# Decode attention with a gated MLP: all heads' scores of a batch in two PSUM banks, one softmax per batch

## The chip, the cores and the metric

One core of a Trainium2 chip runs the whole kernel. The metric is the device time of one execution in microseconds (us). The engines are PE (matmul and transpose), DVE, ACT, POOL and SP, which here only issues the loads.

## What is computed

Four sequences (B) with one token each, width 576 (D). 32 query heads share 16 key/value heads (KVH) of size 128, two query heads to one. Attention looks at the last 4096 positions (WIN) of a cache of 16384. All inputs are bf16.

```python
h  = x + softmax(q @ k.T * DH**-0.5) @ v @ wo        # q = layernorm(x) @ wq, per batch and head
g  = layernorm(h) @ W_gate                           # 576 x 4608
h2 = h + (relu(g) * (layernorm(h) @ W_up)) @ W_down  # 4608 x 576
```

K and V of the window are 64 pairs (batch, kv head) of 1 MB each; with the weights (wq, wo, gate, up, down, 4.5 to 5.3 MB each) the core reads 159.58 MB.

## The kernel before

The loop runs over the 64 pairs. For a pair `i`, K arrives as 128 partitions of 32 rows of 128 values. `do_tr` (line 582) transposes its 32 blocks on PE into four PSUM banks of 8 blocks each; `evac` (line 332) copies each bank to `kT_pool`, three on DVE (line 342) and the fourth on ACT (line 344). `do_qk` (line 601) has the blocks of kT as stationary operand and two columns of q as moving one: 32 matmuls of 2 columns, so the scores lie with positions on partitions, 128 x 64 in a bank. `dve_rmax` (line 469) reduces them to 128 x 2, POOL makes the maximum over partitions with `partition_all_reduce` (line 427) and scales it (line 429), `act_exp` (line 384) makes the exponentials of each of the two heads with that bias. `do_pv` (line 622) has the blocks of V as stationary operand and two columns of probabilities as moving one: 32 matmuls at line 633.

PE's order for step `i` is: transposes of pair i, QK of pair i-1, PV of pair i-3. The transposes into a bank wait for that bank's copy of the pair before; ACT's queue holds the copy of pair i and then the exponentials of pair i-1. POOL's two instructions per pair stand in order on its queue.

All loads go through SP's queue in one order: x, wq in five chunks of 128 (the last of 64) input rows, then K(m) and V(m-3) alternating, the four parts of wo among them, then gate and up by chunks of input rows, then down in five parts. K, wq, gate and up share a ring of 7 slots, V and down another of 7; a load waits for the instruction that reads the slot's last content (`add_transfer`, line 237). A wait at the head of SP's queue holds all later loads.

After the loop come `wo` (160 matmuls with 4 columns, line 661), the second layernorm, gate and up (360, line 682), the product, down (180, line 699), a transpose back and one output DMA (line 353).

Of the kernel before, what the change touches and what calls it, by code (L numbers as in the profile page):

```python
# [7 lines left out]
ALU = mybir.AluOpType  # L8
# [4 lines left out]
B = 4  # L13
# [6 lines left out]
T = WIN // 128  # L20
F = 4608
FC = F // 128
# [5 lines left out]
NSTREAM = 14  # L28
NWO = 4
SLOT = 4608  # L30
NKT = 3
NSB = 2
LAGQ = 1
LAGP = 2
NP = 4
NM = 4
NRA = 7
VLEAD = 3
WO_AFTER = 4
KT_BANK0 = 4  # L40
EVAC_ENG = ("vector", "vector", "vector", "scalar")

# [7 lines left out]
class Ev:  # L50
    __slots__ = ("key", "val")

    def __init__(self, key, val):
        self.key = key
        self.val = val


class Sched:
    def __init__(self):
        self.emit = False  # L60
        self.sem_keys = []
        self._keyset = set()
        self.sems = {}
        self.engines = {}
        self.named = {}
        self.rec_hist = {}
        self.begin_pass(False)
        for e in ENGS:
            self._key("cnt_" + e)

    def _key(self, key):
        if key not in self._keyset:
            assert not self.emit, ("semaphore key discovered in emit pass", key)
            self._keyset.add(key)
            self.sem_keys.append(key)

    def begin_pass(self, emit, nc=None, es=None):
        self.emit = emit
        self.counters = {e: 0 for e in ENGS}
        self.dma_counts = {}  # L80
        self.waited = {}
        self.rec_idx = {}
        if not emit:
            self.rec_hist = {}
            self.named = {}
        else:
            for key in self.sem_keys:
                self.sems[key] = es.enter_context(nc.semaphore("s_" + key))
            self.engines = {
                "sync": nc.sync,  # L90
                "scalar": nc.scalar,
                "vector": nc.vector,
                "gpsimd": nc.gpsimd,
                "tensor": nc.tensor,
            }

    def record(self, name, ev):
        if self.emit:
            idx = self.rec_idx.get(name, 0)
            self.rec_idx[name] = idx + 1  # L100
            hist = self.rec_hist.get(name)
            assert hist is not None and idx < len(hist), ("event not seen in pass 1", name)
            old = hist[idx]
            assert old.key == ev.key and old.val == ev.val, ("event mismatch", name)
        else:
            self.rec_hist.setdefault(name, []).append(ev)
        self.named[name] = ev
        return ev

    def get(self, name):  # L110
        ev = self.named.get(name)
        if ev is None:
            if self.emit:
                raise KeyError(name)
            return None
        return ev

    def wait(self, eng, ev):
        if ev is None:
            return  # L120
        k = (eng, ev.key)
        if self.waited.get(k, -1) >= ev.val:
            return
        self.waited[k] = ev.val
        if self.emit:
            self.engines[eng].wait_ge(self.sems[ev.key], ev.val)

    def op(self, eng, thunk, deps=()):
        for d in deps:
            self.wait(eng, d)  # L130
        key = "cnt_" + eng
        self._key(key)
        self.counters[eng] += 1
        val = self.counters[eng]
        if self.emit:
            ins = thunk(self.engines[eng])
            ins.then_inc(self.sems[key], 1)
        return Ev(key, val)

    def dma(self, eng, thunk, sem_key, deps=(), val=None):  # L140
        for d in deps:
            self.wait(eng, d)
        self._key(sem_key)
        self.dma_counts[sem_key] = self.dma_counts.get(sem_key, 0) + 16
        if val is None:
            val = self.dma_counts[sem_key]
        if self.emit:
            ins = thunk(self.engines[eng])
            ins.then_inc(self.sems[sem_key], 16)
        return Ev(sem_key, val)  # L150


def bass_sequential_preLN__sliding_block_cached__glu_gated_reglu__decode_kernel(
# [12 lines left out]
    with ExitStack() as es:  # L166
        cnt = [0]

        def sb(shape, dt):
            cnt[0] += 1  # L170
            return es.enter_context(nc.sbuf_tensor(f"sbt{cnt[0]}", shape, dt))

        def ps(shape, dt):
            cnt[0] += 1
            return es.enter_context(nc.psum_tensor(f"pst{cnt[0]}", shape, dt))

        pool = sb([128, NSTREAM + NWO, SLOT], BF16)
        kT_pool = sb([128, NKT, WIN], BF16)
        ident_b = sb([128, 128], BF16)
        ident_f = sb([128, 128], FP32)  # L180
        ones_f = sb([128, 128], FP32)
        eps_c = sb([128, 1], FP32)
        x_bf = sb([B, D], BF16)
        x_f = sb([B, D], FP32)
        junk_f = sb([B, D], FP32)
        xn_bf = sb([B, D], BF16)
        st1 = sb([B, 16], FP32)
        xnT = sb([128, DC, B], BF16)
        xT = sb([128, DC, B], FP32)
        qT_sb = sb([128, B, H], BF16)  # L190
        pmax = sb([128, NM, 2], FP32)
        bcm = sb([128, NM, 2], FP32)
        nb = sb([128, NM, 2], FP32)
        probT = sb([128, NP, T, 2], BF16)
        rowsum = sb([128, B, H], FP32)
        rs_sb = sb([128, H], FP32)
        oT_all = sb([128, H, B], BF16)
        R_sb = sb([128, 2, DC, B], FP32)
        st2 = sb([128, 40], FP32)
        tmp5 = sb([128, DC, B], FP32)  # L200
        hnT = sb([128, DC, B], BF16)
        acc = sb([128, 2, FC, B], FP32)
        hhT = sb([128, FC, B], BF16)
        h2T = sb([128, DC, B], FP32)
        out_sb = sb([B, D], BF16)

        pb = [ps([128, 512], FP32) for _ in range(8)]
        tpv = pb[1][:, :].bitcast(BF16)
        qps = pb[0]
        ktbv = [pb[KT_BANK0 + j][:, :].bitcast(BF16) for j in range(4)]  # L210
        SC_BANK0 = 0
        OT_BANK0 = 2

        S = Sched()

        def knat(s):
            return pool[:, s, 0:WIN].rearrange("p (t d) -> p t d", d=DH)

        def kTview(ks):
            return kT_pool[:, ks, :].rearrange("d (t p) -> d t p", p=128)  # L220

        def vview(s):
            return pool[:, s, 0:WIN].rearrange("p (t d) -> p t d", d=DH)

        def woview(g):
# [531 lines left out]
```

## Time and profile before

| | us |
|---|---|
| median of 3 runs | 1054.41 |
| lowest and highest | 1052.48, 1055.69 |
| span of the profiled execution | 1053.8 |

The times of the rows come from that one profiled execution, counted from its first instruction. A matmul group's busy time holds overlapping instructions once. PEclk is the share of PE's full clock that was granted: 0.50 is 1.2 GHz and 1.00 is 2.4 GHz. DMA is the mean busy share of the 16 DMA engines. "issue" is time for which the profile shows no releaser.

### The profile page before, as it was taken

What the parts mean: (1) busy time and instruction counts of PE and PEld (TensorE: products, weight loads), DVE (VectorE), ACT (ScalarE), POOL (GpSimd) and SP (SyncE); (2) the same over time, 40 slices, a digit from 0 to 9 for tenths busy, and PEclk for the clock granted to TensorE, in tenths of its full rate; (3) what the DMA queues carried; (4) which work ended last, traced back from release to release, by engine and by line L of the source; (5) the groups of instructions that cost most, each with busy time, mean ns of one, the idle gap of its engine ahead of it and who ended that gap; (6) DMA issues with size and microseconds to landing.
All of it is one profiled execution on the core that took longest, in us unless ns stands there. A gap on an engine that the chain in (4) does not pass through costs nothing.

```text
span 1053.8 us, 15473 instructions
## 1 busy us (share of the span) xinstructions
PE 378.8 (36%) x7029; PEld 358.8 (34%) x7029; DVE 155.4 (15%) x299; ACT 108.2 (10%) x333; POOL 41.2 (4%) x138
## 2 busy tenths in 40 slices
PE   3622432343234323432442344324432443243156
PEld 3511332333233323332332233223332333232156
DVE  0310111111111111101110111011111111110010
ACT  2100111011101110111011001100111011011000
POOL 0000000000000000000000000000000000000000
PEclk9755555555555555555555555555555555555555
DMA  7994533443344234423433443234323441532027
GB/s 260 383 411 179 202 110 134 160 160 118 123 160 160 104 137 161 160 97 143 160 130 114 158 160 138 106 156 160 143 104 153 160 157 44 199 106 90 1 68 227
DMA packets 29331, 160.59 MB, mean 152 GB/s; under 512 B 2441, under 2 KB 11153, under 8 KB 11153
## 3 DMA queue, kind: packets, MB, share of 16 engines
q1 hardware_dynamic: 29264, 159.60, 40.2%
q8 instruction: 55, 0.90, 0.3%
q14 instruction: 12, 0.09, 0.0%
HBM read 159.58 MB, written 0.00 MB: 151 GB/s over the span
## 4 chain that ended last, share of the span: by engine, by line
issue 58%; PE 21%; ACT 9%; POOL 4%; DVE 3%; DMA 2%; POOLq 1%; SPq 1%; ACTq 0%; DVEq 0%
PE pst L595 10%; ACT sbt L344 5%; PE pst L616 5%; ACT sbt L384 4%; PE pst L633 3%; POOL sbt L427 2%; DVE sbt L342 2%; POOL sbt L429 2%; DMA sbt<-in_A_wq_dram 1%; DMA sbt<-in_B_W_down_dram 1%; PE pst L574 1%; SPq L318 1%; POOLq L166 1%; DVE sbt L469 1%; PE pst L661 1%
## 5 line engine op out<-in xcount | busy, mean ns | idle before, releaser
L595 PE MATMUL pst<-sbt 128*128 128x128 bf16 x2048 | 235.8, 308 | 609.7 <-ACT sbt L344 609.7
L595 PEld LDWEIGHTS pst<-sbt 128*128 128x128 bf16 x2048 | 205.2, 144 | 625.7 <-ACT sbt L344 625.7
L342 DVE COPY sbt<-pst 128x1024 bf16<-128x1024 bf16 x192 | 132.3, 691 | 95.8 <-PE pst L595 95.7
L384 ACT ACTIVATE sbt<-pst,sbt 128x32 bf16<-128x32 f32 x128 | 36.3, 294 | 874.8 <-POOL sbt L429 874.8
L469 DVE TENSOR_REDUCE sbt<-pst 128x2 f32<-128x64 f32 x64 | 14.4, 225 | 710.1 <-PE pst L633 709.0
L633 PE MATMUL pst<-sbt 128*128 128x2 bf16 x2048 | 63.5, 165 | 24.6 <-ACT sbt L384 24.6
L616 PEld LDWEIGHTS pst<-sbt 128*128 128x128 bf16 x2048 | 67.3, 107 | 10.7 <-ACT sbt L384 10.5
L616 PE MATMUL pst<-sbt 128*128 128x2 bf16 x2048 | 66.4, 166 | 10.6 <-ACT sbt L384 10.5
L633 PEld LDWEIGHTS pst<-sbt 128*128 128x128 bf16 x2048 | 59.6, 104 | 24.7 <-issue 24.7
L344 ACT COPY sbt<-pst 128x1024 bf16<-128x1024 bf16 x64 | 64.6, 1009 | 24.8 <-PE pst L595 23.5
L427 POOL PARTITION_ALL_REDUCE sbt<-sbt x64 | 23.8, 372 | 417.7 <-issue 209.3
L429 POOL TENSOR_SCALAR sbt<-sbt 128x2 f32<-128x2 f32 x64 | 16.1, 251 | 546.4 <-issue 546.4
L384 ACT ACTIVATION_READ_ACCUMULATOR sbt<-pst,sbt 128x1 f32 x128 | 25.1, 196 | 0.0
L682 PE MATMUL pst<-sbt 128*128 128x4 bf16 (+1 forms) x360 | 10.9, 165 | 8.4 <-issue 6.2
L682 PEld LDWEIGHTS pst<-sbt 128*128 128x128 bf16 (+1 forms) x360 | 10.7, 103 | 8.7 <-issue 6.4
L574 PE MATMUL pst<-sbt 128*128 128x4 bf16 (+1 forms) x160 | 10.1, 173 | 9.1 <-DMA sbt<-in_A_wq_dram 9.1
L699 PE MATMUL pst<-sbt 128*128 128x4 bf16 (+1 forms) x180 | 12.6, 180 | 1.4 <-DVE sbt L542 1.2
L574 PEld LDWEIGHTS pst<-sbt 128*128 128x128 bf16 (+1 forms) x160 | 9.1, 105 | 10.1 <-issue 9.1
L699 PEld LDWEIGHTS pst<-sbt 128*128 128x128 bf16 (+1 forms) x180 | 11.4, 112 | 2.6 <-DMA sbt<-in_B_W_down_dram 1.5
L661 PE MATMUL pst<-sbt 128*128 128x4 bf16 (+1 forms) x160 | 5.5, 172 | 0.7 <-DVE sbt L478 0.7
L661 PEld LDWEIGHTS pst<-sbt 128*128 128x128 bf16 (+1 forms) x160 | 5.3, 115 | 0.9 <-DVE sbt L478 0.8
L476 DVE RECIPROCAL sbt<-pst 128x32 f32<-128x32 f32 x4 | 1.4, 350 | 27.6 <-PE pst L639 27.6
(62 smaller groups left out, 27.2 us busy)
## 6 DMA issues: line engine op xcount, KB each, us to landing
sbt<-in_A_k_cache_dram SPq DMA_DIRECT2D x64, 1024.0 KB, 5.0
sbt<-in_A_v_cache_dram SPq DMA_DIRECT2D x64, 1024.0 KB, 6.4
sbt<-in_A_wo_dram SPq DMA_DIRECT2D x4, 1152.0 KB, 19.2
sbt<-in_B_W_gate_dram SPq DMA_DIRECT2D x4, 1152.0 KB, 7.7
sbt<-in_B_W_up_dram SPq DMA_DIRECT2D x4, 1152.0 KB, 5.7
sbt<-in_B_W_down_dram SPq DMA_DIRECT2D x4, 1152.0 KB, 13.4
sbt<-in_A_wq_dram SPq DMA_DIRECT2D x4, 1024.0 KB, 7.9
sbt<-in_B_W_gate_dram SPq DMA_DIRECT2D x1, 576.0 KB, 8.9
```

The source lines that it names most:

```text
L342: ev = S.op(eng, lambda e, dst=dst, srcv=srcv: e.tensor_copy(out=dst, in_=srcv), deps=deps)
L344: ev = S.op(eng, lambda e, dst=dst, srcv=srcv: e.copy(out=dst, in_=srcv), deps=deps)
L384: ev = S.op(a, lambda e, j=j, psl=psl, scv=scv, mi=mi, b=b, kvh=kvh: e.activation(out=probT[:, psl, :, j], in_=scv[:, j, :], func=ACT.Exp, ...
L427: ev = S.op(g, lambda e, mi=mi: e.partition_all_reduce(bcm[:, mi, :], pmax[:, mi, :], 128, bass_isa.ReduceOp.max), deps=deps)
L429: ev = S.op(g, lambda e, mi=mi: e.tensor_scalar(out=nb[:, mi, :], in0=bcm[:, mi, :], scalar1=-SCALE, scalar2=None, op0=ALU.mult), deps=[ev])
L469: ev = S.op(v, lambda e, mi=mi, sbk=sbk: e.tensor_reduce(out=pmax[:, mi, :], in_=pb[sbk][:, 0:2 * T].rearrange("p (t h) -> p h t", h=2), a ...
L574: ev = S.op(t, lambda e, h=h, c=c, w=w, s=s: e.matmul(qps[:, h * B:(h + 1) * B], lhsT=pool[0:w, s, h * DH:(h + 1) * DH], rhs=xnT[0:w, c, : ...
L595: ev = S.op(t, lambda e, j=j, u=u, tt=tt, kn=kn: e.transpose(out=ktbv[j][:, u * 128:(u + 1) * 128], in_=kn[:, tt, :], identity=ident_b[:, :]),
L616: ev = S.op(t, lambda e, tt=tt, kt=kt, sbk=sbk, b=b, kvh=kvh: e.matmul(pb[sbk][:, 2 * tt:2 * tt + 2], lhsT=kt[:, tt, :], rhs=qT_sb[:, b, 2 ...
L633: ev = S.op(t, lambda e, tt=tt, vv=vv, ob=ob, kvh=kvh, psl=psl: e.matmul(ob[:, 2 * kvh:2 * kvh + 2], lhsT=vv[:, tt, :], rhs=probT[:, psl, ...
L682: ev = S.op(t, lambda e, bank=bank, col=col, w=w, s=s, f=f, c=c: e.matmul(bank[:, col:col + B], lhsT=pool[0:w, s, f * 128:(f + 1) * 128], ...
L699: ev = S.op(t, lambda e, n=n, w=w, wv=wv, j=j, fc=fc: e.matmul(pb[n][0:w, 0:B], lhsT=wv[:, j, n * 128:n * 128 + w], rhs=hhT[:, fc, :], sta ...
```

## The change

The scheduler that went over the program twice is replaced by one that records operations per engine and emits them with their waits (`Prog`); only instructions that someone waits for increment a semaphore.

- **QK.** K is transposed as before. The stationary operand is now q, 32 columns of it: `qTm[:, b, kvh, :]` holds the two heads of kv head `kvh` in their columns and zeros in the other 30. The moving operand is kT, 512 columns at once. Eight matmuls per pair: four groups `j` of 1024 positions write the four 32-partition strips of banks 4 and 5 (the four column groups of PE). All 16 kv heads of a batch accumulate in these two banks: the masked columns add zeros.
- **Softmax.** Once per batch: DVE takes the maximum of each of the 128 rows (strip j, head) over 1024 columns, ACT the exponentials of 128 x 1024 with the sum. The four strips of a head have maxima of their own; `weights` works out a factor for each strip by two small matmuls, four small DVE operations and a small exponential, and the sum of a head's strips by a third matmul. POOL has no part in the loop.
- **PV.** The probabilities of a batch are transposed (8 transposes) and copied into `pTm`, masked like q. The stationary operand is 32 columns of it, the moving one a block of V: 32 matmuls of 128 columns per pair, group j to strip j of bank 6, all pairs of a batch accumulating. `finish_o` joins the strips with a matmul on the factors.
- **Order.** PE's step s: at a batch's start the 8 transposes of the probabilities, then transposes of K(s), QK of pair s-2, PV of pair s-19. Four copies of kT per pair, two on DVE and two on ACT.
- **Loads.** On SP: K 0 and 1, wq, then K alone up to 17, then K(s) and V(s-18) alternating, in one ring of 16 slots; wo as one load after V 57, over the space of kT and of the first slots, so that it waits for the last QK and for PV 49; then the last six V, gate and up, down in four parts of 1152 rows (contiguous 10 KB per partition), the last two over the space of wo. x goes on ACT's queue.
- **The rest.** wq, wo, gate/up and down have activations (padded to 32 columns) as stationary operand and weights as moving one, in four column groups: 40 matmuls of 512 columns, 64 of 288, 120 of 384, 144 of 144. The residual is added by matmuls into down's bank; the output goes out in four DMAs.

The diff, cut to its core:

```diff
-                ev = S.op(g, lambda e, mi=mi: e.partition_all_reduce(bcm[:, mi, :], pmax[:, mi, :], 128, bass_isa.ReduceOp.max),
-                          deps=deps)
-                ev = S.op(g, lambda e, mi=mi: e.tensor_scalar(out=nb[:, mi, :], in0=bcm[:, mi, :], scalar1=-SCALE, scalar2=None,
-                                                             op0=ALU.mult),
-                          deps=[ev])
...
-                    ev = S.op(t, lambda e, tt=tt, kt=kt, sbk=sbk, b=b, kvh=kvh: e.matmul(
-                        pb[sbk][:, 2 * tt:2 * tt + 2], lhsT=kt[:, tt, :], rhs=qT_sb[:, b, 2 * kvh:2 * kvh + 2],
...
+        def add_kv(kind, i):
+            b, kvh = divmod(i, KVH)
+            s = ring_slot()
+            off = slot0 + s * TILE
...
+        for s in range(2):
+            add_kv("K", s)
+        for c in range(DC):
+            add_wq(c)
+        for s in range(2, NPAIR):
+            add_kv("K", s)
+            if s >= VDMA_LAG:
+                add_kv("V", s - VDMA_LAG)
...
+        def evac(i, j):
...
+            if j % 2 == 0:
+                dve(("EV", i, j), lambda e: e.tensor_copy(out=dst, in_=src), deps)
+            else:
+                act(("EV", i, j), lambda e: e.copy(out=dst, in_=src), deps)
...
+        def pe_qk(i):
...
+            for u in range(2):
+                for j in range(4):
...
+                    if j == 0 and kvh == 0:
...
+                            deps += [("EXP", b - 1), ("MAX", b - 1)]
+                    o = pe(("QK", i), lambda e, u=u, j=j: e.matmul(
+                        bank[4 + u][32 * j:32 * j + 32, :], lhsT=qTm[:, b, kvh, :],
+                        rhs=k[:, j * 1024 + u * 512:j * 1024 + (u + 1) * 512],
+                        start=(kvh == 0), stop=(kvh == KVH - 1), skip_group_check=True), deps)
...
+        def dve_max(b):
+            dve(("MAX", b), lambda e: e.tensor_reduce(out=stat[:, b, 0:1], in_=s_ps, axis=AX.X, op=ALU.max, negate=True),
+                [("QK", b * KVH + KVH - 1)])
...
+        def pe_pv(i):
...
+            for tl in range(8):
+                for j in range(4):
...
+                    pe(("PV", i), lambda e, tl=tl, j=j: e.matmul(
+                        o_ps[32 * j:32 * j + 32, 0:DH], lhsT=pTm[:, tl, j, kvh, :], rhs=v[:, 8 * j + tl, :],
+                        start=(kvh == 0 and tl == 0), stop=(kvh == KVH - 1 and tl == 7), skip_group_check=True), deps)
...
+        def weights(b):
+            pe(("MT", b), lambda e: e.matmul(m_ps[0:1, 0:128], lhsT=stat[:, b, 0:1], rhs=ident_f[:, :], start=True, stop=True),
...
+            pe(("MB", b), lambda e: e.matmul(m_ps[:, 0:1], lhsT=gm4[0:1, :], rhs=ones_f[0:1, 0:1], start=True, stop=True),
+               [("GM2", b), "c_ones"])
...
+            pe(("LS", b), lambda e: e.matmul(m_ps[:, 0:32], lhsT=ones_f[:, :], rhs=selw[:, 1, :], start=True, stop=True),
+               [("SELL", b)])
...
+        for s in range(NPAIR + PV_LAG):
+            if s >= PV_LAG and (s - PV_LAG) % KVH == 0:
+                pe_pt((s - PV_LAG) // KVH)
+                put_pT((s - PV_LAG) // KVH)
+            if s < NPAIR:
+                pe_tr(s)
+                for j in range(4):
+                    evac(s, j)
...
+            q = s - QLAG
+            if 0 <= q < NPAIR:
+                pe_qk(q)
+                if q % KVH == KVH - 1:
+                    dve_max(q // KVH)
+                    act_exp(q // KVH)
+            v = s - PV_LAG
+            if 0 <= v < NPAIR:
+                pe_pv(v)
+                b, kvh = divmod(v, KVH)
+                if kvh == 2:
+                    weights(b)
+                if kvh == KVH - 1:
+                    finish_o(b)
```

## Rows read from the trace of the kernel before

**Rows 1.** The page: span, PE's busy time, 40 slices of GB/s, bytes read.

```profile
span 1053.8 us, 15473 instructions
...
PE 378.8 (36%) x7029; PEld 358.8 (34%) x7029; DVE 155.4 (15%) x299; ACT 108.2 (10%) x333; POOL 41.2 (4%) x138
...
GB/s 260 383 411 179 202 110 134 160 160 118 123 160 160 104 137 161 160 97 143 160 130 114 158 160 138 106 156 160 143 104 153 160 157 44 199 106 90 1 68 227
...
HBM read 159.58 MB, written 0.00 MB: 151 GB/s over the span
```

**Rows 2.** Waits: engine and line, for whom, us in total, times, longest.

```profile
ACT sbt L384 <- POOL sbt L429: 874.8, 64, 21.5
...
PE pst L595 <- ACT sbt L344: 609.7, 61, 17.7
...
SPq L260 <- PE pst L616: 675.1, 52, 17.4
```

**Rows 3.** Timeline of one pair: start us, us, engine, line, count, [idle before].

```profile
409.15 1.03 PE L595 MATMUL pst<-sbt 128*128 128x128 bf16 x8 [9.21 <-ACT sbt L344]
...
410.88 0.99 PE L633 MATMUL pst<-sbt 128*128 128x2 bf16 x32
...
411.74 2.72 PE L595 MATMUL pst<-sbt 128*128 128x128 bf16 x24
...
413.69 0.37 POOL L427 PARTITION_ALL_REDUCE sbt<-sbt  x1 [6.17 <-DVE sbt L342]
...
422.48 0.25 POOL L429 TENSOR_SCALAR sbt<-sbt 128x2 f32<-128x2 f32 x1 [8.42 <-issue]
...
428.65 0.37 POOL L427 PARTITION_ALL_REDUCE sbt<-sbt  x1 [5.92 <-issue]
```

**Rows 4.** Timeline: POOL's line 429, the first and the last two of 64.

```profile
45.78 0.25 POOL L429 TENSOR_SCALAR sbt<-sbt 128x2 f32<-128x2 f32 x1 [11.38 <-issue]
...
992.18 0.25 POOL L429 TENSOR_SCALAR sbt<-sbt 128x2 f32<-128x2 f32 x1 [6.76 <-issue]
...
1006.17 0.25 POOL L429 TENSOR_SCALAR sbt<-sbt 128x2 f32<-128x2 f32 x1 [7.14 <-issue]
```

**Rows 5.** Windows: us, busy (count) of PE, PEld, DVE, ACT, POOL, PEclk, DMA, GB/s.

```profile
2.00:3.00 1.00, 0.00 (x0) 0.00 (x0) 0.00 (x0) 0.73 (x2) 0.48 (x3) 1.00 1.03 131
29.00:82.00 53.00, 18.86 (x356) 18.15 (x353) 11.62 (x21) 6.41 (x13) 1.62 (x5) 0.62 1.02 414
...
1028.00:1031.00 3.00, 1.67 (x63) 1.59 (x60) 0.46 (x1) 0.00 (x0) 0.00 (x0) 0.50 0.89 181
```

**Rows 6.** Timeline of the end: the last matmuls on wd, the output's DMA.

```profile
1045.38 4.22 PE L699 MATMUL pst<-sbt 128*128 128x4 bf16 x60 [0.15 <-DMA sbt<-in_B_W_down_dram]
...
1052.14 0.29 SPq L353 DMA_DIRECT2D out_dram<-sbt  x1
```

**Rows 7.** Timeline: 32 transposes while the granted clock was 1.00.

```profile
33.17 1.95 PE L595 MATMUL pst<-sbt 128*128 128x128 bf16 x32
```

**Rows 8.** The page's costliest groups: line, shapes, count, busy us, mean ns, idle.

```profile
L595 PE MATMUL pst<-sbt 128*128 128x128 bf16 x2048 | 235.8, 308 | 609.7 <-ACT sbt L344 609.7
...
L342 DVE COPY sbt<-pst 128x1024 bf16<-128x1024 bf16 x192 | 132.3, 691 | 95.8 <-PE pst L595 95.7
...
L469 DVE TENSOR_REDUCE sbt<-pst 128x2 f32<-128x64 f32 x64 | 14.4, 225 | 710.1 <-PE pst L633 709.0
...
L344 ACT COPY sbt<-pst 128x1024 bf16<-128x1024 bf16 x64 | 64.6, 1009 | 24.8 <-PE pst L595 23.5
```

**Rows 9.** Windows with the granted clock in the column PEclk.

```profile
26.60:36.50 9.90, 9.90 (x175) 9.89 (x175) 6.59 (x12) 3.31 (x3) 0.38 (x1) 1.00 0.87 343
...
107.30:112.60 5.30, 5.30 (x96) 5.04 (x96) 1.61 (x3) 0.00 (x0) 0.37 (x1) 0.50 0.60 210
113.20:116.70 3.50, 0.00 (x0) 0.00 (x0) 0.13 (x1) 0.00 (x0) 0.00 (x0) 0.98 1.02 396
...
1036.80:1049.60 12.80, 12.61 (x180) 11.36 (x180) 0.00 (x0) 0.00 (x0) 0.00 (x0) 0.50 0.71 255
```

More of the change, by code (lines that the diff above doesn't have):

```diff
@@ new lines, in bass_sequential_preLN__sliding_block_cached__glu_gated_reglu__decode_kernel, with place @@
+        mb_ps = bankb[7]
+        owner = {}
+        land = {}
+        uses = {}
+        def place(name, off, size, reader, make, key=None):
+            deps = []
+            for blk in range(off // 64, (off + size) // 64):
+                r = owner.get(blk)
+                if r is not None and r not in deps:
+                    deps.append(r)
+                owner[blk] = reader
+            semk = key or "d_" + "_".join(str(v) for v in name)
+            P.dma("sync", ("L",) + name, make, semk, deps)
+            land[name] = off
@@ L727, in bass_sequential_preLN__sliding_block_cached__glu_gated_reglu__decode_kernel @@
-        for name, p in progs:
-            getattr(block, name)(lambda e, p=p: p(S))
+                off = land[("wq", c)]
+                for n in range(8):
+                    g, bk = n % 4, n // 4
+                    pe("QMM", lambda e, c=c, w=w, off=off, n=n, g=g, bk=bk: e.matmul(
+                        bank[4 + bk][32 * g:32 * g + 32, :], lhsT=xnT[0:w, c, :], rhs=arena[0:w, off + n * 512:off + (n + 1) * 512],
+                        start=(c == 0), stop=(c == DC - 1), skip_group_check=True),
+                        ([("L", "wq", c)] + (["xnT", "c_xnT"] if c == 0 else [])) if n == 0 else [])
@@ new lines, in act_q, with pe_tr @@
+        def act_q():
+            act("qev1", lambda e: e.copy(out=p_sb[:, 512:1024], in_=bank[5]), ["QMM"])
+        def pe_tr(i):
+            kn = kv("K", i)
+            for j in range(4):
+                for u in range(8):
+                    t = j * 8 + u
+                    deps = []
+                    if u == 0:
+                        deps = [("L", "K", i)] if j == 0 else []
+                        if i == 0:
+                            deps.append("c_idb")
+                        else:
+                            deps.append(("EV", i - 1, j))
+                    last = j == 3 and u == 7
+                    o = pe(("TRJ", i, j), lambda e, j=j, u=u, t=t: e.transpose(
+                        out=bankb[TRB[j]][:, u * 128:(u + 1) * 128], in_=kn[:, t, :], identity=ident_b[:, :]), deps)
+                    if last:
+                        P.names[("TR", i)] = o
@@ new lines, in bass_sequential_preLN__sliding_block_cached__glu_gated_reglu__decode_kernel @@
+        dve("part0", lambda e: e.tensor_copy(out=part[:, 0:288], in_=bank[0][:, 0:288]), ["WO", ("PV", NPAIR - 1)])
+        act("part1", lambda e: e.copy(out=part[:, 288:576], in_=bank[1][:, 0:288]), ["WO", ("PV", NPAIR - 1)])
+        for c in range(DC):
+            w = _dw(c)
+            pe("HT", lambda e, c=c, w=w: e.matmul(m_ps[0:w, c * 4:(c + 1) * 4], lhsT=part[:, c * 128:c * 128 + w], rhs=sel4[:, 0:4],
+                                                  start=True, stop=True), ["part0", "part1", "c_sel"] if c == 0 else [])
```

989 lines of the change are left out of this document (377 added, 612 removed).

## The prediction

> **What bounds the kernel now.** I read the page first [rows 1]. The span is 1053.8 us, PE is busy for 36% of it, and the core reads 159.58 MB. In the third of the 40 slices the loads moved 411 GB/s; in most later ones 90 to 200. So neither PE nor the DMA engines are full, and something makes both wait. The waits name it in a chain [rows 2]: ACT waits 874.8 us for POOL's line 429, PE waits 609.7 us for ACT's line 344, and SP, which issues the loads, waits 675.1 us for PE to free slots. To see whether this is a loop over all engines or one engine, I read one pair in order of time [rows 3]. POOL's all-reduce of the maximum (line 427) starts at 413.69 us, and its follower, line 429, at 422.48. Then POOL stands idle for 5.92 us, released by nothing that the profile shows (its column says issue), and starts the next all-reduce: its own two instructions per pair cost it the period. The end bears this out: when PE has only PV left to do, the last two of line 429 still lie 14.0 us apart [rows 4]. From the first line 429 (45.78 us) to the 64th (1006.17 us) it is 960.4 us for 63 periods, 15.2 us each. The span is thus 46 us of start, 960 us of POOL, 48 us of tail.
>
> **The change, part by part.** POOL's two instructions leave the loop: all 960 us of that bound go. What is late next is either the loads or PE; I cost both.
>
> *Loads.* The bytes stay the same, 159.58 MB [rows 1]. The longest stretch in which the DMA engines were full moved 414 GB/s over 53 us, with loads of wo in it [rows 5], and the third slice of the page, 26 us, moved 411 [rows 1]. I take 411, the lower, because the new stream would have to last seven times longer: 159.58 / 0.411 = 388.3 us. Loads into 64 partitions are dearer: gate and up's last chunks moved 181 GB/s with the engines 0.89 busy [rows 5]. There are three such (0.52 + 2 x 0.59 = 1.70 MB): 9.4 us instead of 4.1, so 5.3 more. The stream starts at about 2.7 us, since the third microsecond moved 0.131 MB, a third of what a full one moves [rows 5]. It ends at 2.7 + 388.3 + 5.3 = 396.3 us, if it never starves. After the last wd chunk come 36 matmuls of the down projection; the old kernel's last 60 took 4.22 us [rows 6]; four column groups side by side would do 9 x 0.13 = 1.2 us, one after another 4.7; I take 1.2. The output copy is some 0.3, and the output DMA needs 1.7 to the span's end as now (1052.14 to 1053.8) [rows 6]. Span 399.5. The median of runs lies 0.6 us over the profiled span (1054.41 against 1053.8), and the tail's semaphores add some tenths: 401 us.
>
> *Does it starve?* The ring has 16 slots for K and V. K(s) takes the slot of K(s-8), V(s-18) that of V(s-26), so SP waits for PE's step s-8 only: PE may be seven steps late before a load waits. One instruction is different: SP is one queue, and the load of wo waits for the last QK (step 65) and for PV 49 (step 68), with six V and all MLP weights queued behind it. At full rate PV 49 can run at 305 us, and wo's turn in the stream is at 323, so it costs nothing; if PE is the bound, the stream stops there and 26.9 MB (70 us with its half-partition loads) follow PE's step 68. The waits of wd 2 and 3 for the output projection are reached at about 383 us, some 25 us after it is done: nothing.
>
> *PE.* Each step now streams three times 4096 columns: 32 transposes of 128, QK as 8 matmuls of 512, PV as 32 of 128. The transposes are as before: at the clock of 0.50 eight take 1.03 and 24 take 2.72 us [rows 3], 3.75 a step; at the granted clock of 1.00, 32 took 1.95 [rows 7]. No row shows 32-column groups at work. Bound above: each stream costs as much as the transposes (3.75 or 1.95). Bound below: four groups side by side, a quarter (0.94 or 0.49), and for PV no less than 32 weight loads and matmuls took, 0.99 [rows 3]. I take the lower, because the four groups write different PSUM partitions from different columns of the array. To this come up to three changes between whole-array and grouped matmuls, each between 0 and 0.3 us (a transpose's mean 308 ns from start to end [rows 8]); I take 0.1 each. At the high clock: 1.95 + 0.49 + 0.99 + 0.3 = 3.7 us. The loads give a K and a V (2.10 MB) every 5.1 us, so PE has 1.4 us to spare in each of the 46 steps that load both. In the first 18 steps, with K alone, PE needs 2.7 us against 2.55: even.
>
> The Trainium skill, "TensorEngine Tiling (Array Packing)", Theoretical Speedup and Key Properties, states up to four times for 32 columns, and a drain of the engine when the tiling mode changes. No row here shows either. By it the step would be the one I took, with drains inside my bound.
>
> *Clock.* Ten microseconds of transposes and small matmuls kept the granted clock at 1.00, and a burst of 5.3 us at 0.50, two thirds of it transposes, was followed by 0.98 [rows 9]. A stretch of 12.8 us in which PE was busy with 4-column matmuls throughout stayed at 0.50 [rows 9], so being busy is not enough. The new PE pauses 1.4 us in 5.1 and streams full columns; I take the high clock (2.4 GHz) for most of the stage, and a step that is too slow at the low one (1.2 GHz) only makes PE denser.
>
> *Evacuation.* DVE now makes two and ACT two of the four copies of a pair: 2 x 0.69 = 1.4 and 2 x 1.01 = 2.0 us [rows 8], under the 5.1. PE's next transposes need a bank 2.5 us or more after it was filled: hidden.
>
> *The softmax of a batch* is new. The maximum over 1024 fp32 columns lies between a copy of 1024 (0.69) and 16 times the 64-column reduction of 0.225 (3.6) [rows 8]; the exponential is about ACT's copy of 1024 columns, 1.0. The next batch's first QK waits for both, behind the next transposes: at most 4.6 - 1.95 = 2.7 us of PE. The weights of the four groups add two stops of PE (line MB behind three small DVE operations, LS behind DVE, ACT, DVE, DVE), each behind one copy in its queue: at most 2 us each. PV of that step and all transposes queue behind them. About 7 us of PE per batch, against seven steps of head start (36 us): nothing, as long as the loads are the bound; 28 us in all if PE is.
>
> **The rivals.**
>
> *A, the low clock throughout, groups side by side.* For it: 12.8 busy us at 0.50 [rows 9], and that a 32-column group may count for little. Against it: the transposes alone held 1.00 [rows 9]. Step 3.75 + 0.94 + 0.99 + 0.3 = 6.0. PE starts step 2 at 25 us (K 0, K 1 and wq, 6.8 MB, are there at 20.6, then q is copied and transposed); 16 steps of 4.8 (no PV) reach 102, 46 of 6.0 reach 378, five short ones 386; then 70 us of loads and 5 us of end: 461. Drains of 0 and 0.3 give 444 and 499. The Trainium skill, "TensorE: Matmul & The Clock Gate", Part 4, says that transposes do not count as work for the full clock; by it this rival, 461, would hold. Row 26.6 to 36.5 of [rows 9], mostly transposes at 1.00, speaks against the rule.
>
> *B, the groups run one after another, at the high clock.* For it: no row shows them together. Step 3 x 1.95 + 0.3 = 6.15; K-only 4.2; start at 30, since wq's 20480 columns take 9.7 us. 30 + 67 + 46 x 6.15 = 380, 15 for five steps, 70 loads, 5 end: 470.
>
> *C, B at the low clock.* 11.6 and 7.8 a step: 37 + 125 + 534 + 27 = 723, then 70 to 115 us, as the MLP's columns are serial too: 800 to 840.
>
> *D, slower than before.* Successive matmuls lie in different groups; if each waited until the one before had left the array, QK, PV, wq, wo, gate/up and down (2928 matmuls) would cost p each instead of a share of a stream. Transposes 240, longer matmuls' extra columns 231, start and end 20, so 491 + 2928 p: at p = 0.308 us [rows 8] it is 1393. It is slower than before from p = 0.192 us. Against it: fresh weights and a matmul every 31 ns now (0.99 / 32) [rows 3].
>
> **How the numbers follow.** Forecast 0.65, A 0.12, B 0.12, C 0.06, D 0.02; the remaining 0.03 is a stream that does not hold its rate. The time is 401. The forecast's own range is 390 (393 at 414 GB/s with the loads into 64 partitions as cheap as the rest, and some us for a purer stream of K and V) to 415 (some 14 us of small stops). To hold 8 in 10 the range takes in A's and B's middle, so 390 to 470. About 0.3% is what a measurement of this kernel can tell (its runs span 1052.48 to 1055.69); faster is all but D and an unknown of the same size: 0.97, same 0.01, slower 0.02.
>
> **What would show it.** Right: DMA 9 tenths in every slice from the second to the last but one and some 410 GB/s; PE waiting for K loads; no POOL in the chain; QK's eight matmuls within 0.5 to 1 us; PE's clock at 1.00 in most slices. Wrong: SP waiting for PE (A to C), QK's eight in 1.9 us or more (B), in 3.7 at the low clock (C), a transpose step that starts late behind grouped matmuls 0.2 us apart (D). Were the wq stage serial, the first step with K alone would be past 35 us.

## The result and the profile after

The changed kernel takes 403.57 us (median; 403.25 to 404.20), before 1054.57 in the same comparison: a ratio of 0.382 (0.381 to 0.383). The forecast was 401. Lines of the page of the changed kernel (PEclk and DMA in tenths per slice of 10 us):

```profile
span 402.3 us, 10840 instructions
...
PE 265.4 (66%) x5091; PEld 209.7 (52%) x5091; DVE 121.9 (30%) x218; ACT 138.3 (34%) x154; POOL 3.9 (1%) x21
...
PEclk9866999999888889888889897988886555566556
DMA  8999999999999999999999999999999999999992
GB/s 321 372 402 422 419 419 419 419 418 421 419 418 421 419 420 419 421 419 418 419 420 419 420 419 420 416 421 419 421 419 419 412 367 370 425 422 415 209 360 118
...
DMA 67%; PE 19%; SPq 9%; DVE 3%; issue 1%; ACT 0%
```

Against [rows 1]: the DMA engines are 8 or 9 tenths busy in every slice but the last, at 419 GB/s in most, and POOL has gone from the chain. The weak slices are the first two, the two at 370 (wo), and the last three. The waits (us in total, times, longest) have turned round: PE now waits for the load of K, and SP for PE only as its ring fills.

```profile
PE psb L373 <- DMA sb_arena<-in_A_k_cache_dram: 53.8, 35, 5.8
```

One step of PE and the start of the next, from the timeline; the first row belongs to an earlier step:

```profile
207.19 2.51 PE L373 MATMUL psb<-sb_ident_b,sb_arena 128*128 128x128 bf16 x32 [2.01 <-DMA sb_arena<-in_A_k_cache_dram]
...
212.16 1.96 PE L373 MATMUL psb<-sb_ident_b,sb_arena 128*128 128x128 bf16 x32 [0.63 <-DMA sb_arena<-in_A_k_cache_dram]
214.04 0.62 PE L402 MATMUL psb<-sb_arena,sb_qTm 128*32 128x512 bf16 x8
214.49 0.62 PE L452 MATMUL psb<-sb_arena,sb_pTm 128*32 128x128 bf16 x32
217.13 1.96 PE L373 MATMUL psb<-sb_ident_b,sb_arena 128*128 128x128 bf16 x32 [2.02 <-DMA sb_arena<-in_A_k_cache_dram]
```

The step of 212.16 has its transposes, QK and PV done after 2.95 us; then PE waits 2.02 us for K. Windows of the same trace (columns as in [rows 5]):

```profile
40.00:80.00 40.00, 39.04 (x667) 30.64 (x665) 23.39 (x35) 31.67 (x34) 0.00 (x0) 1.00 1.01 419
100.00:300.00 200.00, 147.36 (x2920) 121.96 (x2920) 63.62 (x105) 79.50 (x84) 0.00 (x0) 0.85 1.01 419
...
209.00:210.00 1.00, 1.00 (x11) 0.57 (x13) 0.58 (x1) 0.57 (x2) 0.00 (x0) 0.50 0.98 410
...
318.00:330.00 12.00, 4.18 (x128) 3.11 (x128) 0.00 (x0) 0.00 (x0) 0.00 (x0) 0.50 1.05 395
330.00:336.00 6.00, 0.00 (x0) 0.00 (x0) 0.00 (x0) 0.00 (x0) 0.00 (x0) 0.50 0.81 275
...
372.00:384.00 12.00, 2.81 (x32) 0.89 (x36) 0.00 (x0) 0.00 (x0) 0.00 (x0) 0.51 1.02 210
392.00:398.00 6.00, 2.16 (x100) 1.78 (x92) 0.00 (x0) 0.00 (x0) 0.00 (x0) 0.78 0.53 220
```

The end, against [rows 6]: the last 36 down matmuls start when the last load lands.

```profile
398.38 1.27 PE L593 MATMUL psb<-sb_arena,sb_pTm 128*32 128x144 bf16 x36 [2.34 <-DMA sb_arena<-in_B_W_down_dram]
399.70 0.31 DVE L596 CAST sb_out_sb<-psb 128x144 bf16<-128x144 f32 x1 [8.24 <-PE psb L593]
400.04 0.67 SPq L600 DMA_DIRECT2D out_dram<-sb_out_sb  x2
```

### The profile page after: what moved, and what is told of

Same layout as the page of the kernel before. It is cut to its first block, busy times and chain, and to the rows that moved or that the text cites. A ratio compares the mean times of both kernels' runs of the same rounds, so it can differ in the third digit from the quotient of the medians.

```text
span 402.3 us, 10840 instructions
## 1 busy us (share of the span) xinstructions
PE 265.4 (66%) x5091; PEld 209.7 (52%) x5091; DVE 121.9 (30%) x218; ACT 138.3 (34%) x154; POOL 3.9 (1%) x21
## 3 DMA queue, kind: packets, MB, share of 16 engines
HBM read 159.58 MB, written 0.00 MB: 397 GB/s over the span
## 4 chain that ended last, share of the span: by engine, by line
DMA 67%; PE 19%; SPq 9%; DVE 3%; issue 1%; ACT 0%
DMA sb_arena<-in_A_k_cache_dram 42%; PE psb L373 13%; DMA sb_arena<-in_A_v_cache_dram 11%; DMA sb_arena<-in_B_W_down_dram 10%; SPq L225 8%; DMA sb_arena<-in_A_wq_dram 4%; PE psb L402 3%; DVE sb_pTm L496 2%; PE psb L452 1%; PE psb L518 1%; SPq L232 1%; PE psb L593 0%; DVE sb_stat L410 0%; ACT sb_p_sb L416 0%; PE psb L331 0%
## 5 line engine op out<-in xcount | busy, mean ns | idle before, releaser
L373 PE MATMUL psb<-sb_ident_b,sb_arena 128*128 128x128 bf16 x2048 | 151.9, 243 | 60.4 <-DMA sb_arena<-in_A_k_cache_dram 53.8
L373 PEld LDWEIGHTS psb<-sb_ident_b,sb_arena 128*128 128x128 bf16 x2048 | 140.1, 111 | 74.2 <-DMA sb_arena<-in_A_k_cache_dram 60.2
L387 ACT COPY sb_arena<-psb 128x1024 bf16<-128x1024 bf16 x128 | 125.4, 1014 | 143.2 <-PE psb L373 143.2
L385 DVE COPY sb_arena<-psb 128x1024 bf16<-128x1024 bf16 x128 | 87.9, 690 | 152.0 <-PE psb L373 151.7
L452 PE MATMUL psb<-sb_arena,sb_pTm 128*32 128x128 bf16 x2048 | 49.2, 251 | 32.7 <-DMA sb_arena<-in_A_v_cache_dram 31.5
L452 PEld LDWEIGHTS psb<-sb_arena,sb_pTm 128*32 128x32 bf16 x2048 | 41.6, 113 | 50.7 <-DMA sb_arena<-in_A_v_cache_dram 35.5
L402 PE MATMUL psb<-sb_arena,sb_qTm 128*32 128x512 bf16 x512 | 44.0, 425 | 1.0 <-ACT sb_p_sb L416 1.0
L560 PE MATMUL psb<-sb_arena,sb_hnT 128*32 128x384 bf16 (+1 forms) x120 | 10.2, 500 | 14.8 <-DMA sb_arena<-in_B_W_up_dram 8.4
L402 PEld LDWEIGHTS psb<-sb_arena,sb_qTm 128*32 128x32 bf16 x512 | 8.1, 97 | 9.0 <-issue 3.3
L496 DVE MEMSET sb_pTm<- 128x8192 uint32 x1 | 6.9, 6885 | 1.6 <-issue 1.6
L593 PEld LDWEIGHTS psb<-sb_arena,sb_pTm 128*32 128x32 bf16 x144 | 3.2, 121 | 4.8 <-DMA sb_arena<-in_B_W_down_dram 4.6
```

Of the source, the lines that this page charges most:

```text
L373: o = pe(("TRJ", i, j), lambda e, j=j, u=u, t=t: e.transpose(out=bankb[TRB[j]][:, u * 128:(u + 1) * 128], in_=kn[:, t, :], identity=ident_ ...
L385: dve(("EV", i, j), lambda e: e.tensor_copy(out=dst, in_=src), deps)
L387: act(("EV", i, j), lambda e: e.copy(out=dst, in_=src), deps)
L402: o = pe(("QK", i), lambda e, u=u, j=j: e.matmul(bank[4 + u][32 * j:32 * j + 32, :], lhsT=qTm[:, b, kvh, :], rhs=k[:, j * 1024 + u * 512:j ...
L452: pe(("PV", i), lambda e, tl=tl, j=j: e.matmul(o_ps[32 * j:32 * j + 32, 0:DH], lhsT=pTm[:, tl, j, kvh, :], rhs=v[:, 8 * j + tl, :], start= ...
L496: dve("c_pTm", lambda e: e.memset(pflat, 0.0))
```

## The experiments

The theory: POOL bound the old kernel, the stream of loads bounds the new one, PE has room. Times are medians; ratios are to the kernel before.

### Was it POOL alone?

```diff
-                ev = S.op(g, lambda e, mi=mi: e.partition_all_reduce(bcm[:, mi, :], pmax[:, mi, :], 128, bass_isa.ReduceOp.max),
+                ev = S.op(g, lambda e, mi=mi: e.tensor_copy(out=bcm[:, mi, :], in_=pmax[:, mi, :]),
```

> The kernel before, with POOL's all-reduce over partitions replaced by a POOL copy of the 128 x 2 maxima: the maximum over partitions is left out, each partition keeps its own, all else stays (QK and PV with two columns, three copies on DVE, the old loads). Theory (POOL's 15.2 us per pair were the only bound, the loads are next): the 960 us of the loop fall to the loads' 64 x 5.0 = 320 us; start (46 us, with a stop of the loads at 20 to 28 us) and tail (48 us, partly loads) stay: about 430 us, between 410 and 450. Rival (PE's order with its waits for ACT's copy behind the exponentials is nearly as bad): 64 steps of 8 to 10 us, 600 to 730 us. Were it over 700, grouped matmuls and not POOL would be what the change is worth.

Measured: 418.51 us, 0.397 (0.396 to 0.398). The old kernel without the all-reduce is as full of loads as the new one in all but the third slice and the end, with 2-column matmuls and all:

```profile
PE 326.1 (78%) x7029; PEld 318.4 (76%) x7029; DVE 150.7 (36%) x299; ACT 114.8 (28%) x333; POOL 26.7 (6%) x138
...
GB/s 312 343 122 417 421 410 421 409 421 411 418 420 418 421 417 420 420 417 418 420 417 417 420 418 420 417 420 417 420 420 417 420 417 420 418 378 282 222 345 23
...
L595 PE MATMUL pst<-sbt 128*128 128x128 bf16 x2048 | 182.1, 270 | 47.9 <-DMA sbt<-in_A_k_cache_dram 47.5
```

Of the 651 us that the change brings, 636 come with this one operation. PE's side of the old kernel was no bound: it is busy for 78% of the span here, and still waits 47.5 us for K. The copy gives a wrong maximum; what a right one without POOL would have cost in the old layout was not tried.

The 15 us that are left: the third slice above, where K 2 waits for the q projection, and the end. One word moves wq:

```diff
-            add_transfer(("wq", c), "A", "wq", "QDONE",
+            add_transfer(("wq", c), "B", "wq", "QDONE",
```

> The kernel before without the all-reduce over partitions (the maximum over partitions is left out, as in the run above), and with wq loaded into the ring of V instead of that of K, so that K 2 to 6 need not wait for the q projection. Theory (of the 15 us between that run and the kernel after, half is the stop of the loads in its first 30 us, 122 GB/s in one slice of 10 us, and half its end): the stop goes, 7 us less than 418.5: 411 to 412. Rival (the stop only moves the loads, and PE, which had 78% to do, is late all the same): 416 to 419.

Measured: 410.73 us, 0.390 (0.388 to 0.392). 7.8 us come back; where the other 7 lie was not tried. From 20 to 30 us the loads now move 421 GB/s; without the edit it was 85:

```profile
20.00:30.00 10.00, 10.00 (x141) 9.35 (x141) 2.03 (x4) 0.00 (x0) 0.00 (x0) 1.00 1.02 421
```

Is the all-reduce's period POOL's own, or once round a loop of engines?

```diff
+                          if i % 2 else e.tensor_copy(out=bcm[:, mi, :], in_=pmax[:, mi, :]),
```

> The kernel before with POOL's all-reduce over partitions only for every second pair (the others keep each partition's own maximum, so this part of the softmax is left out there). Theory (the 15.2 us are POOL's own time for one all-reduce, in which it works for nobody else and waits for nobody): a pair with and a pair without it take 15.2 + 0.5 us together, 32 x 15.7 = 502 us of loop and 94 us of start and tail, less what the loads take over of these: 560 to 600. Rival (15.2 us are once round a loop of POOL, ACT, PE and DVE, which each pair has to go round, in 5 us where the all-reduce is missing): 32 x 20.2 + 94 = 740.

Measured: 639.92 us, 0.608 (0.604 to 0.612): between the two. POOL in the middle of that run:

```profile
324.98 0.25 POOL L430 TENSOR_SCALAR sbt<-sbt 128x2 f32<-128x2 f32 x1 [10.33 <-issue]
...
325.56 0.21 POOL L430 TENSOR_SCALAR sbt<-sbt 128x2 f32<-128x2 f32 x1
331.81 0.37 POOL L427 PARTITION_ALL_REDUCE sbt<-sbt  x1 [6.03 <-DVE sbt L342]
341.22 0.25 POOL L430 TENSOR_SCALAR sbt<-sbt 128x2 f32<-128x2 f32 x1 [9.04 <-issue]
```

The gap before an all-reduce is 6.03 us, as it was 5.92 in [rows 3], and the pair without one adds 0.5 us to POOL. In this run the row maximum comes only 2.6 us ahead of the all-reduce, so a part of a loop could hide in the gap. The old kernel excludes that for itself. Its 64th and last row maximum ends at 981.10 us, and the 64th all-reduce starts at 998.66, 6.23 us after POOL's line before it:

```profile
980.88 0.22 DVE L469 TENSOR_REDUCE sbt<-pst 128x2 f32<-128x64 f32 x1 [12.15 <-PE pst L633]
...
998.66 0.37 POOL L427 PARTITION_ALL_REDUCE sbt<-sbt  x1 [6.23 <-issue]
```

From the second pair on, every row maximum of that trace lay ready 15 us or more before its all-reduce. POOL waited for nobody: the gap is its own time.

But what follows the all-reduce is not a constant: 9.0 here and 10.3 in the period before, 8.4 in the old kernel's middle, 11.4 at its start and 7 at its end [rows 3, 4]. It is longer where the loads are denser. Two of these stretches in the old kernel, in which the other engines did next to nothing, are 13.03 us long, up to 68.81 us, with the loads at 408 GB/s, and 7.14 us, up to 1006.17, with no loads [rows 4]:

```profile
55.00:69.00 14.00, 0.00 (x0) 0.00 (x0) 0.00 (x0) 0.00 (x0) 0.56 (x2) 0.50 1.02 408
...
993.00:1007.00 14.00, 0.99 (x32) 0.93 (x32) 0.00 (x0) 0.65 (x6) 0.62 (x2) 0.50 0.00 0
```

That the loads lengthen it is read from these rows, not tried by itself. My sum had taken 15.2 us as a constant. Over this run a pair with and a pair without the all-reduce take 17.25 us together (line 430 from 57.05 to 591.87 us, 31 times), and 32 x 17.25 + 94 = 646 comes near the time.

### Has PE room?

```diff
+                    if u % 2 == 0:
+                        pe(None, lambda e, j=j, u=u, t=t: e.transpose(
+                            out=bankb[TRB[j]][:, u * 128:(u + 1) * 128], in_=kn[:, t, :], identity=ident_b[:, :]), deps)
+                        deps = []
```

> The kernel after, with every second transpose of K issued twice (16 more matmuls of 128 columns per pair). Theory (the loads bound the time and PE has some 1.4 us to spare per pair): 16 more cost 0.95 us per pair at the high clock, a step of 4.1 us under the loads' 5.0; the time stays within 2 us of 403.6. Rival (PE's steps with their stops are the bound, and the busy DMA only looks like it): 64 x 0.95 = 61 us more, about 464.

Measured: 405.37 us, 0.384 (0.383 to 0.386). 1024 more transposes cost 1.8 us, not 61. PE's busy share of the middle rose from 147 to 176 us of 200, the rate stayed:

```profile
100.00:300.00 200.00, 176.06 (x3906) 153.38 (x3898) 69.80 (x119) 90.21 (x94) 0.00 (x0) 0.97 1.01 419
```

The same without the line `if u % 2 == 0`:

> The kernel after, with every transpose of K issued twice (32 more per pair, 1.9 us at the high clock). Theory: the step becomes 3.1 + 1.9 = 5.0 us, as long as the loads' 5.0, and the steps with K alone 4.4; the slack is just used up, so some 5 to 20 us more than 403.6 (409 to 424), from the stops that no slack hides any longer. Rival (PE is the bound already): 64 x 1.9 = 122 us more, about 525. If PE had much more slack than 1.4 us, no change.

Measured: 430.41 us, 0.408 (0.406 to 0.411). More than I gave. The page shows three places, in slices of 10.7 us:

```profile
GB/s 326 358 412 419 422 418 421 415 370 246 278 387 343 418 419 415 420 419 413 341 343 415 421 418 420 419 415 356 376 423 416 408 55 388 429 424 420 320 337 181
```

First the loads fall where V begins, with PE busy throughout; against 419 GB/s these 30 us lose 9.

```profile
90.00:120.00 30.00, 30.00 (x572) 26.72 (x572) 11.85 (x18) 14.70 (x16) 0.00 (x0) 1.00 0.77 289
```

I had looked for the loss in the steps with K and V. This part comes from the steps with K alone: a load lands there every 2.5 us, PE takes it up every 4.2, as SP's issues show, and the ring is used up.

```profile
97.08 0.33 SPq L225 DMA_DIRECT2D sb_arena<-in_A_k_cache_dram  x1
101.31 0.33 SPq L225 DMA_DIRECT2D sb_arena<-in_A_v_cache_dram  x1
105.53 0.33 SPq L225 DMA_DIRECT2D sb_arena<-in_A_k_cache_dram  x1
```

Afterwards a step with K and V takes 4.7 us, under the 5.0 of its two loads. But where a batch's weights stop PE, the slack no longer hides it (387 and 343, 341 and 343, 356 and 376 in the page's row): together another 9 us. From QK to QK such a step takes 9.99 us (201.70 to 211.69); PE stands three times, and then 31 of its 64 transposes are 0.107 us apart instead of 0.056 (the granted clock from 206.4 to 211.7 us is 0.68).

```profile
201.49 0.22 PE L373 MATMUL psb<-sb_ident_b,sb_arena 128*128 128x128 bf16 x1
201.55 0.22 PE L376 MATMUL psb<-sb_ident_b,sb_arena 128*128 128x128 bf16 x1
201.70 0.62 PE L405 MATMUL psb<-sb_arena,sb_qTm 128*32 128x512 bf16 x8
...
206.15 0.41 PE L476 MATMUL psb<-sb_selw,sb_ones_f 128*128 128x32 f32 x2 [0.97 <-DVE sb_selw L474]
```

Third, SP waits at the load of wo for PE's PV (the slice at 55): some 8 us more are lost there than in the changed kernel.

```profile
SPq L255 <- PE psb L455: 14.6, 1, 14.6
```

Column groups:

```diff
-                        bank[4 + u][32 * j:32 * j + 32, :], lhsT=qTm[:, b, kvh, :],
+                        bank[4 + u][32 * (j if kvh == 0 else 0):32 * (j if kvh == 0 else 0) + 32, :], lhsT=qTm[:, b, kvh, :],
...
-                        o_ps[32 * j:32 * j + 32, 0:DH], lhsT=pTm[:, tl, j, kvh, :], rhs=v[:, 8 * j + tl, :],
+                        o_ps[32 * (j if tl == 0 else 0):32 * (j if tl == 0 else 0) + 32, 0:DH], lhsT=pTm[:, tl, j, kvh, :], rhs=v[:, 8 * j + tl, :],
```

> The kernel after, with QK (from the second kv head of a batch on) and PV (28 of its 32 matmuls) all writing the first 32-partition strip, so that one column group does nearly all of the work; the scores and outputs are not the reference's. Theory (four groups stream side by side): one after another QK takes 8 x 0.216 = 1.7 and PV some 1.75 us instead of 0.62 each at the high clock; the step becomes 1.9 + 1.7 + 1.75 + 0.3 = 5.7 us, more than the loads' 5.0, and the time about 445 (430 to 460). Rival (the groups are served one after another anyway and only start early): QK and PV as long as now, 403 to 406.

Measured: 440.45 us, 0.418 (0.416 to 0.420). In one group QK and PV take 3.45 us from 205.07 to 208.52, with the four groups 1.00 (153.29 to 154.29, in the dense step of the run with half loads below):

```profile
205.07 1.47 PE L402 MATMUL psb<-sb_arena,sb_qTm 128*32 128x512 bf16 x6
206.17 0.23 PE L452 MATMUL psb<-sb_arena,sb_pTm 128*32 128x128 bf16 x3
206.38 0.59 PE L402 MATMUL psb<-sb_arena,sb_qTm 128*32 128x512 bf16 x2
206.81 1.78 PE L452 MATMUL psb<-sb_arena,sb_pTm 128*32 128x128 bf16 x29
208.52 1.96 PE L373 MATMUL psb<-sb_ident_b,sb_arena 128*128 128x128 bf16 x32
```

So the groups do stream side by side. The Trainium skill, "TensorEngine Tiling (Array Packing)", Theoretical Speedup, gives up to four times for 32 columns; these rows come to 3.5. QK alone takes 1.74 us (205.07 to 206.81) against 0.44, which is 3.95 times, and PV 1.71 against 0.56, three times.

How low does PE's own bound lie?

```diff
-            src = (A_k_cache if kind == "K" else A_v_cache)[b, kvh, SK - WIN:SK, :].rearrange("(p t) d -> p (t d)", p=128)
+            src = (A_k_cache if kind == "K" else A_v_cache)[b, kvh, SK - WIN:SK, :].rearrange("(p t) d -> p (t d)", p=128)[:, 0:TILE // 2]
...
-                        out=bankb[TRB[j]][:, u * 128:(u + 1) * 128], in_=kn[:, t, :], identity=ident_b[:, :]), deps)
+                        out=bankb[TRB[j]][:, u * 128:(u + 1) * 128], in_=kn[:, t % 16, :], identity=ident_b[:, :]), deps)
```

> The kernel after, with only half of each K and V loaded (the first 16 of the 32 rows per partition, 0.5 MB a load); PE, DVE and ACT do all their work, each half read twice, so the output is not the reference's. Theory (the loads bound the kernel after, PE's steps of 3.1 us at the high clock are the next bound): 67 MB less is 160 us less of stream, but PE then needs 35 us to step 3, 15 x 2.44 to step 18, 46 x 3.1 and 16 us of stops between batches, and some 70 us of weights and end remain after that: 295 to 310. If only the loads counted: 403.6 - 160 = 244. If PE were the bound now: unchanged, near 403.

Measured: 312.83 us in the faster of two runs (317.72 in the other), a little over the expected range and 69 over what the loads alone would give. A dense step there takes 2.89 us; the first row is a step behind a batch's weights:

```profile
144.27 3.32 PE L373 MATMUL psb<-sb_ident_b,sb_arena 128*128 128x128 bf16 x32
...
151.40 1.96 PE L373 MATMUL psb<-sb_ident_b,sb_arena 128*128 128x128 bf16 x32
153.29 0.61 PE L402 MATMUL psb<-sb_arena,sb_qTm 128*32 128x512 bf16 x8
153.73 0.62 PE L452 MATMUL psb<-sb_arena,sb_pTm 128*32 128x128 bf16 x32
154.29 1.96 PE L373 MATMUL psb<-sb_ident_b,sb_arena 128*128 128x128 bf16 x32
```

And the ring's head start:

```diff
-        ring = [(-DC - 2 * NPAIR) % NSLOT]
+        ring = [(-DC - 2 * NPAIR) % 8]
...
-        WO_OFF = 0
-        GU_OFF = H * D
-        WD_OFF = GU_OFF + 10 * F
+        WO_OFF = slot0 + 8 * TILE
+        GU_OFF = 0
+        WD_OFF = WO_OFF + H * D
```

> The kernel after with a ring of 8 slots for K and V instead of 16 (the weights are laid out behind it so that wo waits for nothing). A load waits for what PE does three steps before, not seven. Theory (the stops of PE at a batch's end and its weights are some 7 us, and three steps are 15 us): the loads are not held, 402 to 406. Rival (the head start of seven steps is what hides the stops and the softmax of a batch): 4 x 7 = 28 us more, 425 to 435.

Measured: 404.37 us, 0.384 (0.383 to 0.386). Three steps of head start do as well as seven, for PE as it is in the changed kernel.

### What the stream still loses

```diff
+                      lambda e: e.dma_start(out=arena[0:64, off:off + 2048], in_=A_wq[512:576, 0:2048]), key=f"slot{s}")
+                P.dma("sync", ("L", "wq", 5), lambda e: e.dma_start(out=arena[64:128, off:off + 2048], in_=A_wq[512:576, 2048:4096]),
...
+                make = lambda e, m=m, g=g, W=W, off=off: e.dma_start(out=arena[64 * g:64 * g + 64, off + m * 2304:off + (m + 1) * 2304],
+                                                                     in_=W[512:576, m * 2304:(m + 1) * 2304])
```

> The kernel after, with the last 64 input rows of wq, gate and up spread over all 128 partitions: of wq the first half of the columns on partitions 0 to 63 and the second on 64 to 127, gate's rows on 0 to 63 and up's on 64 to 127 in four alternating loads; the matmuls on them read the matching half, with the activations copied there by one small DVE operation each. Theory (loads into 64 partitions run at half the rate and hold up the loads before them, 372 to 385 us at about 217 instead of 419 GB/s, and 16 to 22 us): about 6 us come back at gate and up and 2 at wq, 395 to 398. Rival (two loads on one queue run one after the other, each at half the rate, whichever half they write): no change, 402 to 404.

Measured: 401.73 us, 0.381 (0.380 to 0.381): 1.8 us of the 6 to 8 expected. The slow stretch stays:

```profile
372.00:384.00 12.00, 3.27 (x40) 0.99 (x43) 0.00 (x0) 0.00 (x0) 0.00 (x0) 0.52 1.01 245
```

wo in parts:

```diff
+                place(("wo", g), off, 8 * D, "WO",
+                      lambda e, g=g, off=off: e.dma_start(out=arena[:, off:off + 8 * D].rearrange("p (h n) -> p h n", n=D),
+                                            in_=A_wo[g * 1024:(g + 1) * 1024, :].rearrange("(h p) n -> p h n", p=128)))
```

> The kernel after, with wo loaded in four parts of 8 heads, each between two of the last V, instead of one load of 4.7 MB. Theory (the one load of 4096 rows of 1152 bytes fills the queue, so that the V behind it is issued too late: 252 and 227 GB/s between 330 and 334 us, some 2 us of the stream): 2 us come back, 401 to 402. Rival (the small rows themselves cost it): no change, 403 to 404.

Measured: 404.21 us, 0.383 (0.382 to 0.384): nothing. The dip only moves, to the first of the four (318 to 326 us below). Nor is it SP's wait before wo: in the run with eight slots wo waits for nothing, and from 332 to 334 us the loads moved 225 GB/s there, 227 in the changed kernel.

```profile
318.00:326.00 8.00, 3.13 (x96) 2.33 (x96) 0.00 (x0) 0.00 (x0) 0.00 (x0) 0.50 0.90 337
```

Both edits together:

> Both edits, the 64-row chunks over 128 partitions and wo in four. Theory: the sum of the two, 393 to 396, since both are losses of the same stream. Rival (something else ends last, as PE's tail): the better of the two alone.

Measured: 402.48 us, 0.381 (0.380 to 0.382), as the first alone. So I took away the 64-partition loads altogether: the last 64 rows as one contiguous block over 128 partitions, half p%2 of row p//2 on partition p, and activations that are zero on the partitions of the other parity.

```diff
-                  lambda e: e.dma_start(out=arena[0:w, off:off + H * DH], in_=A_wq[c * 128:c * 128 + w, :]), key=f"slot{s}")
+                  lambda e: e.dma_start(out=arena[:, off:off + (H * DH if c < 4 else H * DH // 2)],
+                                        in_=A_wq[c * 128:c * 128 + w, :] if c < 4 else
+                                        A_wq[512:576, :].rearrange("r (h n) -> (r h) n", h=2)), key=f"slot{s}")
...
+                            bank[3 * g + m][32 * j:32 * j + 32, 0:384], lhsT=hnT[:, c, :] if c < 4 else hnE[:, j // 2, :],
```

> The kernel after, with the last 64 input rows of wq, gate and up each loaded as one contiguous block over all 128 partitions (partition p holds half p%2 of row p//2); the activations of these rows are doubled on partitions and masked by parity, by some small operations on DVE. Theory (a load that writes 64 partitions only is slow by itself, on whichever half, and slows the loads around it, as 372 to 383 us at 205 to 286 GB/s in the run with the halves alternating on one queue): the slow stretches at 18 to 22 and 372 to 384 us go, some 6 + 2 us come back: 394 to 397. Rival (gate, up or what lies near them in the stream is slow for another reason): 402 to 404, with the slow stretch still there.

Measured: 395.05 us, 0.375 (0.373 to 0.377), 8.5 us under the changed kernel and the fastest here. The rows loaded are as long as in the run with the two halves (4608 bytes for gate and up, 4096 for wq), and the changed kernel read them in one block as well; so neither the length nor the order in memory explains it, and the number of partitions is what is left. The slow stretch is gone:

```profile
372.00:384.00 12.00, 7.67 (x129) 3.94 (x125) 2.24 (x5) 1.52 (x4) 0.00 (x0) 0.50 1.01 425
384.00:390.00 6.00, 1.90 (x84) 1.52 (x79) 0.00 (x0) 0.00 (x0) 0.00 (x0) 0.78 0.38 160
```

## Why the prediction was right, step by step

**The bound.** POOL's line 427 was the bound, and its removal is what moved the time: shown by the run without it. That it waited for nobody is shown by the old kernel's trace (row maxima ready 15 us ahead). Masked q, column groups and one softmax a batch are one way to do without the all-reduce; by themselves they and the new order of loads give only the 15 us left. Half of these, 7.8 us, the old kernel got by the order of its first loads.

**The stream.** The mechanism held, and its terms nearly cancelled. The rate is 419, not 411 GB/s: 159.58 / 0.419 = 380.9, 7.4 us less than my term. The 64-partition loads were a mis-sized term: 5.3 us in the sum, 8.5 measured. I had costed only their own bytes; but 12 us at 210 GB/s are 2.5 MB, and gate's and up's two halves have only 1.18: the full loads beside them are slow too. Two losses had no term. Around wo, 18 us move 6.39 MB (12 x 395 + 6 x 275), 2.8 us lost. In the last six us, 220 GB/s, the loads end unevenly: 2.9 us lost. Together 7.4 less and 3.2 + 2.8 + 2.9 more leave 1.5 us: 397.8 instead of 396.3. The last bytes move at 397.5 us, and the last load counts as landed at 398.3 (359.93 + 38.40 in the chain that ended last). After it come 4.0 us to the span's end (3.2 in the sum), above all because the output's DMA takes 2.3 us and not 1.7. The median lies 1.3 us over the profiled span. The 0.6 in the sum was misread: each execution takes some 1.8 us more than its own span (404.20 and 402.3 us here, 1056.68 and 1054.9 in a run of the old kernel), and the profiled ones were slower than the median. So the bound and the path came out as told; that 401 lies within 3 us is partly luck of terms that cancel.

**Starving.** The head start was sized far too carefully: eight slots do it. The load of wo was issued at 307 us, with K and V still ahead of it in the queue, as reckoned. That it stops the stream when PE is late is what the run with twice the transposes shows (14.6 us of waiting).

**PE.** A step is 2.89 us dense, not 3.7 (1.89 + 0.44 + 0.56). The lower bound for QK was right (0.44 us from its start to PV's), but the 0.99 us floor that I set under PV from fresh 128-column weights [rows 3] was wrong: the 32 matmuls with 32-column weights take 0.56 to the start of the next transposes. The change from whole array to groups costs about the 0.1 us that I took: in the run with twice the transposes these start 0.056 us apart, and QK starts 0.15 us after the last of them (201.55 to 201.70). PV has as many columns per group as QK and takes 0.12 us longer; how much of that is the change back is not shown.

**Clock.** High for most of the stage, as forecast, though not 1.00 in most slices: 1.00 from 40 to 80 us, 0.85 in the mean from 100 to 300. After a pause of two us it was now and then 0.50 in the next step (the step of 207.19, window 209 to 210), and it was 0.50 from 318 to 330 us, where PE had only PV to do. In the changed kernel the loads cover this. Where PE is the bound it costs: in the run with half loads the 32 transposes behind a batch's weights take 3.32 us (144.27) instead of 1.96. The Trainium skill, "TensorE: Matmul & The Clock Gate", Part 4, says that transposes do not count for the full clock; they are most of PE's time here, and the 40 us at 1.00 speak against it, as [rows 9] did.

**Softmax of a batch.** DVE's maximum took 1.2 us and ACT's exponential 1.1, PE stopped 1.0 us for them once, and 0.79 and 0.97 for the weights of each batch: within the bounds, and hidden. Not foreseen: PE began step 2 at 24.60 us, as reckoned, but DVE's 6.9 us of zeroing `pTm` at 27 us stand ahead of its copies of that step and hold PE's step 3 until 34.85, after 6.4 us of standing still. The ring covered it. Whether it is a part of the loss in the run with twice the transposes was not tried.

**The rivals.** B falls by QK's eight matmuls in 0.62 us. Its step was costed somewhat high (1.89 + 3.45 = 5.3 us in the run with one group, 6.15 in the sum), and that run's 440 us stand against its 470. A and C fall by the clock, D by the step of 2.89 us.

## What to carry to other kernels

Look for the one operation that sets the period before redesigning around it: replacing it with a copy, at the price of a wrong maximum, showed in one run where 98% of a rewrite's gain came from. When the loads become the bound, the sum is bytes over the rate of the longest full stretch, and the windows below that rate show where to look: here the loads that don't fill all partitions, which gave 8.5 us, then wo and the first and last ten microseconds, which nothing here improved. Test slack by doing some work twice, and read the result stage by stage: here the middle's ordinary steps had two us to give, the stage with K alone hardly any, and the steps with a batch's weights less than two.

## What the runs showed of the hardware

Loads into 64 partitions about halve the rate of the stream (210 GB/s against 419), also when loads into the lower and the upper half alternate on one queue (245 GB/s), and the full loads next to them suffer as well: 1.70 MB in such loads cost 8.5 us. POOL's all-reduce over partitions of 128 x 2 values took about 15 us of POOL's time: some 6 us before the 0.37 us that are booked as busy (9 to 10 at the dense start of the old kernel) and 7 to 13 after them, more where the loads are dense. Four column groups ran 3.95 times as fast as one with 512 moving columns a matmul, and three times with 128. From the last transpose on the whole array to the first matmul in column groups some 0.1 us are lost. Why the loads dip for some six us once at wo, in one load or in four, stays open, and so does the slow end of the stream (220 GB/s in the last six us, 160 in the fastest version).
